# Clamps of four more weight pieces on GpSimd, and the third tile's products of r and k written ahead of the first weight piece

## The chip, the cores and the metric

The program runs on one core of one Trainium2 chip. The metric is the device time of one execution in microseconds (us). The engines are TensorE (PE; PEld is its weight load), VectorE (DVE), ScalarE (ACT), GpSimd (POOL) and SyncE (SP), whose queue issues the DMAs.

## The reference

Three layers follow each other, all in float32, on batch 4 and sequence 768.

```python
# 1: linear attention with a decaying state, per head (8 heads of 48)
for t in range(S):
    cur = einsum('bhd,bhe->bhde', u * k[t], v[t])
    y[t] = einsum('bhd,bhde->bhe', r[t], state + cur)
    state = w * state + einsum('bhd,bhe->bhde', k[t], v[t])
# 2: MLP 384 -> 1024 -> 384 with a 3-tap convolution over time as gate
h = maximum(x @ w_in, 0)
conv_out = sum(conv_w[k] * shifted(h, k) for k in range(3))
x = (h * sigmoid(conv_out)) @ w_out
# 3: layer norm, MLP 384 -> 1536 -> 384, residual
xn = (x - mean) / sqrt(var + 1e-6) * g_ln
out = x + maximum(xn @ w_ch1, 0) @ w_ch2
```

## The kernel before, in words

The 3072 rows are cut into 24 tiles of 128. For a tile, attention scales r and k by tables of powers of w (`rk`), forms scores on TensorE (`dps`), copies them on ScalarE (`aT`) and masks them (on GpSimd for the first six tiles, which are "light"), and multiplies by v into `yps`. For light tiles VectorE also forms `z`, the product of r and k, of which TensorE makes `pa`. A running state (`pst`, `sn`, `sw`, `sbds`) goes from tile to tile, and `kks` are k's scaled rows for it. The output is split into a rounded high part (`xh`, ScalarE) and a remainder (`xl`, VectorE). Three tiles make a block of 384 rows for the first MLP (`moe1_up`, products `psm` and `acc`, eight channel blocks each); `xh` and `xl` need one column of the next tile too, so the first block waits for the fourth tile. The second MLP runs on blocks of 512 rows after that.

All products of the MLPs use three float32r matmuls: high by high, high by low, low by high. The weights must first be split into such halves, piece by piece (22 pieces, a list `wjobs`): a piece `st` of 512 or 768 columns is loaded, ScalarE takes the absolute value of the upper words (`wdec`, in `magnitude`), a **clamp** follows, then VectorE shifts (first step of `decode`), merges twice, ScalarE writes the high part (`wih`, `woh`) and VectorE the low part (`wil`, `wol`). Piece numbers count from 0 in the code: 0 to 2 and 4 to 6 are of `w_in` (512 columns), 3 and 7 to 9 of `w_out` (768), from 10 on those of the second MLP. The clamp's engine is chosen in `ahead` (line 155): VectorE for pieces 0 to 9, GpSimd for the others. `ahead` of the next piece is called when the merges of a piece have been written, so its absolute value and clamp stand early. `wdo` (line 211) writes the next steps of the decoding at a place of the program.

The scheduler may reorder an engine's work, but instructions that go through the `vo`, `ao`, `go`, `pe` and `so` wrappers (class `InOrder`) keep the order in which they are written, on their own engine. The start is written out by hand in `startup` (line 435): `on(n)` writes the next step of tile n. The steps of a light tile end at the `yield` statements of `attn_tile` and `light_tile`: scaling and `z` on VectorE; scores, selects; output products and the copy `xh`; remainder `xl`. So the third `on(0)` writes TensorE's `yps` of the first tile and ScalarE's `xh`, and the first `on(2)` writes `rk` and `z` of the third tile.

Of the kernel before, what the change touches and what calls it, by code (L numbers as in the profile page):

```python
# [50 lines left out]
def body(ctx, tc, r, k, v, w, u, w_in, conv_w, w_out, g_ln, w_ch1, w_ch2, rkT, krv, small, out):  # L51
# [28 lines left out]
    vo = InOrder(nc.vector)  # L80
    ao = InOrder(nc.scalar)
    so = InOrder(nc.sync)
    go = InOrder(nc.gpsimd)
# [35 lines left out]
    def words(st, n):  # L119
        return [st[:, 0:2 * n].rearrange("p (n two) -> p n two", two=2)[:, :, i] for i in range(2)]  # L120

    def magnitude(st, n, engine=go):

        t = ap.tile([128, WN], F32, tag="wd", name="wdec", bufs=2)[:, 0:n]
        ao.activation(out=t, in_=words(st, n)[1].bitcast(F32), func=AF.Abs)
        engine.tensor_scalar(out=t, in0=t, scalar1=W_MIN, scalar2=W_MAX, op0=ALU.max, op1=ALU.min)
        return t

    def decode(st, n, t):

        lo, hi = words(st, n)
        ti = t.bitcast(I32)
        vo.tensor_scalar(out=ti, in0=ti, scalar1=5, scalar2=2, op0=ALU.logical_shift_left,
                         op1=ALU.logical_shift_right)
        yield
        vo.scalar_tensor_tensor(out=ti, in0=lo, scalar=29, in1=ti, op0=ALU.logical_shift_right, op1=ALU.bitwise_or)
        yield
        vo.scalar_tensor_tensor(out=ti, in0=hi, scalar=-(2 ** 30), in1=ti, op0=ALU.bitwise_and, op1=ALU.bitwise_or)
# [3 lines left out]
    def wjob(src, n, hi, lo, scale=None):  # L142

        st, mag = [], []

        def load():
            st.append(io.tile([128, 2 * WN], I32, tag="st" if me >= 4 else "first", name="st", bufs=3 if me >= 4 else 4))
            dst = st[0][:, 0:2 * n]
            if len(src.shape) == 3:
                dst = dst.rearrange("p (a n) -> p a n", a=src.shape[1])  # L150
            so.dma_start(out=dst, in_=src.bitcast(I32))

        def ahead():
            if not mag:
                mag.append(magnitude(st[0], n, vo if me < 10 else go))

        def steps():
            ahead()
            t = mag[0]
            yield from decode(st[0], n, t)  # L160
            if me + 1 < min(len(wjobs), w_loaded[0]):
                wjobs[me + 1][2]()
            if len(src.shape) == 3:
                t = t.rearrange("p (a n) -> p a n", a=src.shape[1])
            kw = {} if scale is None else {"scale": gl[:, scale:scale + 1]}
            ao.activation(out=hi, in_=t, func=AF.Copy, **kw)
            yield
            if scale is None:
                vo.tensor_tensor(out=lo, in0=t, in1=hi.bitcast(F32), op=ALU.subtract)
            else:  # L170
                vo.scalar_tensor_tensor(out=lo, in0=t, scalar=kw["scale"], in1=hi.bitcast(F32),
                                        op0=ALU.mult, op1=ALU.subtract)
        me = len(wjobs)
        wjobs.append((load, steps(), ahead))
        return len(wjobs) - 1

# [28 lines left out]
    def wload(count):  # L205

        while w_loaded[0] < min(count, len(wjobs)):
            wjobs[w_loaded[0]][0]()
            w_loaded[0] += 1

    def wdo(count=1, last=None):

        for _ in range(count):
            while w_done[0] < (len(wjobs) if last is None else last + 1):
                wload(w_done[0] + 3)
                if next(wjobs[w_done[0]][1], "end") != "end":
                    break
                w_done[0] += 1
# [89 lines left out]
    def ordered(n):  # L308
        return (vo, ao, go) if n < EARLY else (nc.vector, nc.scalar, nc.gpsimd)
# [58 lines left out]
    def attn_tile(n):  # L368
        b, i = divmod(n, TPB)
        rk, _, rt, vt, _ = loaded[n]  # L370
        py, py_tag = (ps_c, "acc") if n < EARLY else (ps_a, "pa")

        rT, kT = rk[:, 0], rk[:, 1]
        vo.tensor_tensor(out=rk, in0=rk, in1=trk, op=ALU.mult)
        if n < LIGHT:
            yield from light_tile(n, rk, vt, py, py_tag)
            return
        av = ap.tile([128, H, D], F32, tag="av", name="av", bufs=2)
        v_.tensor_tensor(out=av, in0=kks[:, n % 2, 1, :, 0:D], in1=rt, op=ALU.mult)
        a8 = sp.tile([128, H, 1], F32, tag="a8", name="a8", bufs=2)  # L380
        v_.tensor_reduce(out=a8.rearrange("x (q p) o -> x q (p o)", q=2), in_=av.rearrange("x (p q) d -> x q p d", q=2),
                         axis=AX.X, op=ALU.add)
        aT = ap.tile([128, 2, NP, C], F32, tag="aT", name="aT", bufs=2)
        for h in range(H):
            a_.activation(out=aT[:, h // NP, h % NP, :], in_=ident, func=AF.Copy, scale=a8[:, h, :])
        yield

        dps = dot_products(rT, kT)
        for q in range(2):
            v_.copy_predicated(out=aT[:, q], mask=later.bitcast(I32).unsqueeze(1).to_broadcast([128, NP, C]), data=dps[q])  # L390
        yield

        yps = py.tile([128, KT, C], F32, tag=py_tag, name="yps")
        products(n, yps, rT, vt, aT)
        j = n // TT
        xh, xl = xT[j] if j in xT else new_xT(j)
        sl = slice(1 + (n % TT) * C, 1 + (n % TT) * C + C)
        a_.activation(out=xh[:, :, sl], in_=yps, func=AF.Copy)
        v_.tensor_tensor(out=xl[:, :, sl], in0=yps, in1=xh[:, :, sl].bitcast(F32), op=ALU.subtract)
        load_tile(n + 3)  # L400
        if n + 2 < NT:
            decayed_k(n + 2)
        halos(n, xh, xl)
        finished[0] = n
        yield
# [3 lines left out]
    def state_sum(n):  # L409
        vt = loaded[n][3]  # L410
        if n % TPB != TPB - 1:
            pst = sums[n] = ps_a.tile([128, NP, D], F32, tag="pa", name="pst")
            for h in range(H):
                q0 = 64 * (h % 2)
                pe.matmul(pst[q0:q0 + 64, h // 2, :], lhsT=kks[:, n % 2, 0, h, :], rhs=vt[:, h, 0:D], start=True,
                          stop=True)

    def state_update(n):
        first, last = n % TPB == 0, n % TPB == TPB - 1
        v_, a_, g_ = ordered(n)  # L420
        if not last:
            pst = sums.pop(n)
            sn = ap.tile([PR, NP, D], F32, tag="sn", name="sn")
            if first:
                a_.activation(out=sn, in_=pst[0:PR], func=AF.Copy)
            else:
                v_.tensor_tensor(out=sn, in0=pst[0:PR], in1=state[0], op=ALU.add)
            if n % TPB < TPB - 2:
                state[0] = ap.tile([PR, NP, D], F32, tag="sw", name="sw")
                v_.tensor_tensor(out=state[0], in0=sn, in1=w128.to_broadcast([PR, NP, D]), op=ALU.mult)  # L430
            sb = sbd[(n + 1) % 2]
            a_.activation(out=sb[0:D, :, 0:D], in_=sn[0:D], func=AF.Copy)
            a_.activation(out=sb[64:PR, :, D:2 * D], in_=sn[64:PR], func=AF.Copy)

    def startup():

        tiles = {n: attn_tile(n) for n in range(EARLY + 1)}

        def on(n):
            next(tiles[n], None)  # L440

        decayed = decayed_k
        on(0), decayed(0), on(0)
        on(1), state_sum(0), state_update(0), decayed(1), on(1), state_sum(1)
        wdo(1)
        on(0), on(2), state_update(1), decayed(2)
        wdo(2)
        on(2), state_sum(2), on(0)
        wdo(1)
        on(1), on(3), state_update(2), decayed(3)  # L450
        wdo(2)
        on(3), state_sum(3), on(1)
        wdo(2)
        on(2), state_update(3)
        wdo(3)
        on(2), on(3)
        wdo(1)
        on(3)
        wdo(1)
        on(4), decayed(4)  # L460
        wdo(3)
        return tiles
# [360 lines left out]

    cst = tables()
    feed = attention(startup())
    for _ in conv_weights(cst):
        pass
# [120 lines left out]
```

## Time and profile before

| | |
|---|---|
| time, three runs | 652.41, 653.33 (median), 654.55 us |
| profiled execution | 653.91 us, span 652.2 us |
| mean granted TensorE clock | 0.975 of full |
| busy over the span | PE 627.9, VectorE 421.7, ScalarE 300.8, GpSimd 81.2 us |
| chain that ended last | PE 84%, VectorE 10%, ScalarE 2%, the rest 1% or less each |
| GpSimd clamps | 13, of which 12 have 768 columns; mean 2749 ns |

The table is read with the span in stages: over the whole span TensorE is the fullest engine (96%), but this is a mean over stages. Times in the rows below are microseconds from the start of the span.

### The profile page before, as it was taken

The page shows a single profiled execution, that of the slowest core. Times are in us where ns is not written, and L with a number is a line of the kernel's source. Part 1 is how long each engine was busy: PE and PEld are TensorE (multiplying, and loading weights), DVE is VectorE, ACT ScalarE, POOL GpSimd, SP SyncE. Part 2 cuts the span into 40 slices and gives each one's busy share as a digit, 9 for nine tenths or more (in the row PEclk, how much of TensorE's full clock was granted, in tenths as well). Part 3 has the DMA queues.
Part 4 walks back from the last instruction along what each step waited for, and adds up shares of the span by engine and source line. Part 5 has one row for each costly group of instructions (what it writes and reads, how often), then busy time and mean ns, then how long its engine had stood idle before and what let it go on. Part 6 is the DMA issues. An engine that isn't in the chain of part 4 may idle for free.

```text
span 652.2 us, 11821 instructions
## 1 busy us (share of the span) xinstructions
PE 627.9 (96%) x4803; PEld 572.3 (88%) x4803; DVE 421.7 (65%) x793; ACT 300.8 (46%) x658; POOL 81.2 (12%) x108
## 2 busy tenths in 40 slices
PE   8969879999999999999999999999999999999996
PEld 5768868889999999999999999999999999999995
DVE  6989999999989999968978834314213422422111
ACT  3447677687687877766755511211211211211110
POOL 6312010110020001002115501001000100100000
PEclk8867989999999999999999999999999999999999
DMA  8934644444253524012125103002002001100001
GB/s 231 309 107 156 211 146 125 125 133 159 71 174 118 162 83 137 18 47 88 52 82 171 60 0 98 1 0 98 1 0 83 16 0 50 50 0 19 31 0 54
DMA packets 25296, 56.52 MB, mean 87 GB/s; under 512 B 2961, under 2 KB 15378, under 8 KB 25234
## 3 DMA queue, kind: packets, MB, share of 16 engines
q1 hardware_dynamic: 25234, 55.68, 27.1%
q8 instruction: 40, 0.66, 0.4%
q14 instruction: 22, 0.18, 0.1%
HBM read 46.24 MB, written 9.44 MB: 85 GB/s over the span
## 4 chain that ended last, share of the span: by engine, by line
PE 84%; DVE 10%; ACT 2%; issue 1%; DMA 1%; POOL 1%; SPq 0%; DVEq 0%; ACTq 0%; POOLq 0%
PE acc L77 36%; PE psm L77 36%; PE yps L77 5%; PE dps L77 4%; DVE wdec L77 3%; DVE c L541 2%; PE pst L77 2%; PE pxt L77 1%; DVE rk L77 1%; DMA x1b<-x_dram 1%; DVE c L522 1%; PE pa L77 1%; DVE gl L528 1%; DVE kks L77 0%; POOL tables L762 0%
## 5 line engine op out<-in xcount | busy, mean ns | idle before, releaser
L555 DVE SCALAR_TENSOR_TENSOR rl<-psm,rh 128x512 fp32r<-128x512 f32 x72 | 49.6, 689 | 136.0 <-ACT rh L554 132.5
L554 ACT ACTIVATE rh<-psm 128x512 fp32r<-128x512 f32 x72 | 43.1, 599 | 199.6 <-PE psm L77 199.5
L77 PE MATMUL acc<-c2h,rh 128*128 128x384 f32 x288 | 97.0, 337 | 0.0
L77 PE MATMUL acc<-c2l,rh 128*128 128x384 f32 x288 | 97.0, 337 | 0.0
L77 PE MATMUL acc<-c2h,rl 128*128 128x384 f32 x288 | 96.9, 336 | 0.0
L77 PE MATMUL psm<-xnh,c1h 128*128 128x512 f32 x216 | 86.6, 401 | 0.0
L77 PE MATMUL psm<-xnh,c1l 128*128 128x512 f32 x216 | 84.9, 393 | 0.0
L77 PE MATMUL psm<-xnl,c1h 128*128 128x512 f32 x216 | 84.7, 392 | 0.0
L541 DVE SCALAR_TENSOR_TENSOR c<-h,tables,c 128x384 f32<-128x384 f32 x128 | 78.5, 617 | 8.0 <-ACT c L539 7.5
L77 PE MATMUL psm<-xh,wih 128*128 128x386 f32 x192 | 69.8, 364 | 4.4 <-DVE xl L77 4.4
L77 PE MATMUL acc<-woh,gl 128*128 128x384 f32 x192 | 65.3, 340 | 4.4 <-DVE gl L528 4.4
L77 PE MATMUL acc<-woh,gh 128*128 128x384 f32 x192 | 67.4, 351 | 0.4 <-ACT gh L527 0.4
L77 PE MATMUL psm<-xl,wih 128*128 128x386 f32 x192 | 67.1, 350 | 0.0
L77 PE MATMUL psm<-xh,wil 128*128 128x386 f32 x192 | 66.9, 348 | 0.0
L77 PE MATMUL acc<-wol,gh 128*128 128x384 f32 x192 | 65.3, 340 | 0.0
L77 PEld LDWEIGHTS acc<-c2l,rh 128*128 128x128 f32 x288 | 54.0, 188 | 3.0
L77 PEld LDWEIGHTS acc<-c2h,rh 128*128 128x128 f32 x288 | 54.1, 188 | 2.8
L77 PEld LDWEIGHTS acc<-c2h,rl 128*128 128x128 f32 x288 | 54.0, 188 | 0.0
L77 PEld LDWEIGHTS psm<-xnh,c1l 128*128 128x128 f32 x216 | 40.6, 188 | 9.3
L77 POOL TENSOR_SCALAR wdec<-wdec 128x768 f32<-128x768 f32 (+1 forms) x13 | 35.7, 2749 | 103.4 <-ACT wdec L77 76.3
L77 PEld LDWEIGHTS psm<-xnl,c1h 128*128 128x128 f32 x216 | 40.6, 188 | 6.1
L77 PEld LDWEIGHTS psm<-xnh,c1h 128*128 128x128 f32 x216 | 40.6, 188 | 6.1
(132 smaller groups left out, 1107.9 us busy)
## 6 DMA issues: line engine op xcount, KB each, us to landing
rk<-in_rkT_dram SPq DMA_DIRECT2D x24, 448.0 KB, 4.5
st<-in_moe_w_ch_dram SPq DMA_DIRECT2D x12, 768.0 KB, 4.6
rv<-in_krv_dram SPq DMA_DIRECT2D x18, 448.0 KB, 4.7
kt<-in_krv_dram SPq DMA_DIRECT2D x24, 192.0 KB, 4.5
x_dram<-x SPq DMA_DIRECT2D x24, 192.0 KB, 1.9
x1b<-x_dram SPq DMA_DIRECT2D x24, 192.0 KB, 3.3
out_dram<-x1b SPq DMA_DIRECT2D x24, 192.0 KB, 2.0
st<-in_moe_w_in_dram SPq DMA_DIRECT2D x6, 512.0 KB, 9.4
```

Source lines behind the costliest of these rows:

```text
L77: return lambda *args, **kw: tc.keep_in_program_order(op(*args, **kw))
L522: v_.tensor_tensor(out=st["c"], in0=st["h"][:, 1:T + 1], in1=st["c"], op=ALU.mult)
L528: v_.tensor_tensor(out=st["gl"], in0=st["c"], in1=st["gh"].bitcast(F32), op=ALU.subtract)
L541: v_.scalar_tensor_tensor(out=c, in0=h[:, o:o + T], scalar=cw[:, tap, f:f + 1], in1=c, op0=ALU.mult, op1=ALU.add)
L554: a_.activation(out=gh[:, 0:cols], in_=ps[:, 0:cols], func=AF.Relu)
L555: v_.scalar_tensor_tensor(out=gl_[:, 0:cols], in0=ps[:, 0:cols], scalar=0.0, in1=gh[:, 0:cols].bitcast(F32), op0=ALU.max, op1=ALU.subtract)
```

## The change

The limit in `ahead` goes from 10 to 6, so that the clamps of pieces 6, 7, 8 and 9 are written for GpSimd. In `startup`, `on(0), on(2)` move from behind `wdo(1)`, which writes the first steps of the first piece, to the place in front of it.

```diff
@@ -152,7 +152,7 @@
 
         def ahead():
             if not mag:
-                mag.append(magnitude(st[0], n, vo if me < 10 else go))
+                mag.append(magnitude(st[0], n, vo if me < 6 else go))
 
         def steps():
             ahead()
@@ -442,8 +442,9 @@
         decayed = decayed_k
         on(0), decayed(0), on(0)
         on(1), state_sum(0), state_update(0), decayed(1), on(1), state_sum(1)
+        on(0), on(2)
         wdo(1)
-        on(0), on(2), state_update(1), decayed(2)
+        state_update(1), decayed(2)
         wdo(2)
         on(2), state_sum(2), on(0)
         wdo(1)
```

**ScalarE and VectorE at the first piece.** In the program before, ScalarE's order from the second tile's column `a8` on (`wdec_338` is the first piece's absolute value, `xh_364` the first tile's output copy):

```order
L77 ACTIVATE a8_321<-pa8_315 128x8
L77 ACTIVATE wdec_338<-st_142 128x512
L77 ACTIVATE xh_364<-yps_342 128x3x128
L77 ACTIVATE sbds_93<-sn_370 48x4x48 x2
L77 ACTIVATE wdec_379<-st_150 128x512
L77 ACTIVATE wih_94<-wdec_338 128x512
```

And in the changed one, where `wdec_366` is the first piece and `xh_360` the first tile's copy:

```order
L77 ACTIVATE a8_321<-pa8_315 128x8
L77 ACTIVATE xh_360<-yps_338 128x3x128
L77 ACTIVATE wdec_366<-st_142 128x512
L77 ACTIVATE sbds_93<-sn_370 48x4x48 x2
L77 ACTIVATE wdec_379<-st_150 128x512
L77 ACTIVATE wih_94<-wdec_366 128x512
```

The absolute value and the copy have changed places. VectorE at the same place before (the first row of `wdec_338`, x2, is its clamp and its shift; `rk_137` and `z` are the third tile's):

```order
L77 TENSOR_TENSOR kks_92<-kt_131,tables_84 128x8x48
L77 TENSOR_SCALAR wdec_338<-wdec_338 128x512 x2
L77 TENSOR_TENSOR rk_137<-rk_137,tables_84 112x1024
L77 TENSOR_TENSOR z_368<-rk_137 112x512
L77 TENSOR_TENSOR sn_370<-pst_329,sw_300 112x192
L77 TENSOR_TENSOR sw_372<-sn_370,w128_87 112x192
L77 TENSOR_TENSOR kks_92<-kt_138,tables_84 128x8x48
L77 SCALAR_TENSOR_TENSOR wdec_338<-st_142,wdec_338 128x512 x2
```

and in the changed program:

```order
L77 TENSOR_TENSOR kks_92<-kt_131,tables_84 128x8x48
L77 TENSOR_TENSOR rk_137<-rk_137,tables_84 112x1024
L77 TENSOR_TENSOR z_364<-rk_137 112x512
L77 TENSOR_SCALAR wdec_366<-wdec_366 128x512 x2
L77 TENSOR_TENSOR sn_370<-pst_329,sw_300 112x192
L77 TENSOR_TENSOR sw_372<-sn_370,w128_87 112x192
L77 TENSOR_TENSOR kks_92<-kt_138,tables_84 128x8x48
L77 SCALAR_TENSOR_TENSOR wdec_366<-st_142,wdec_366 128x512 x2
```

The third tile's two products stand ahead of the clamp; the rest keeps its order.

**GpSimd from the fifth tile's selects on** (L336; `wdec` with 24 columns are the convolution weights, `va` a product of the light tiles), the difference:

```order
 L294 MEMSET xl 128x3
-L336 AFFINE_SELECT aT<-aT 128x512 x2
+L336 AFFINE_SELECT aT<-aT 128x512
 L77 TENSOR_SCALAR wdec<-wdec 128x24
+L336 AFFINE_SELECT aT<-aT 128x512
 L340 TENSOR_TENSOR va<-rv,a_675 128x384
+L77 TENSOR_SCALAR wdec<-wdec 128x512
+L77 TENSOR_SCALAR wdec<-wdec 128x768
 L336 AFFINE_SELECT aT<-aT 128x512 x2
 L340 TENSOR_TENSOR va<-rv,a_824 128x384
-L77 TENSOR_SCALAR wdec<-wdec 128x768
+L77 TENSOR_SCALAR wdec<-wdec 128x768 x3
```

Four clamps have come in, two of them ahead of the sixth tile's selects, and the small clamp of the convolution weights has moved between the fifth tile's two selects.

**TensorE at the fifth tile's scores** (`dps_659`), behind the first channel block's products. TensorE's order is the same in both programs up to the end of the first MLP; what differs here is what the first score waits for. Before:

```order
L77 MATMUL psm_630<-xl_365,wih_94 128x386
L77 MATMUL psm_630<-xh_364,wil_95 128x386
L77 MATMUL dps_659<-rk_157 128x128 [waits DMAHW1_49,DVE_49,Activation_49]
L77 MATMUL dps_660<-rk_157 128x128
L77 MATMUL dps_659<-rk_157 128x128
```

and now:

```order
L77 MATMUL psm_630<-xl_361,wih_94 128x386
L77 MATMUL psm_630<-xh_360,wil_95 128x386
L77 MATMUL dps_659<-rk_157 128x128 [waits DMAHW1_49,DVE_49]
L77 MATMUL dps_660<-rk_157 128x128
L77 MATMUL dps_659<-rk_157 128x128
```

It no longer waits for ScalarE. Behind all this the scheduler also gives VectorE another order of its work on the first MLP's first three blocks, with the same instructions.

## Rows read from the trace of the kernel before

**Rows 1.** Busy time by stage: us, then busy time of each engine (instructions), PEclk, DMA share, GB/s.

```profile
50.00:90.00 40.00, 33.60 (x313) 30.70 (x313) 39.51 (x65) 31.14 (x66) 7.04 (x6) 0.93 0.50 157
90.00:123.00 33.00, 31.25 (x395) 27.96 (x395) 31.14 (x56) 23.92 (x64) 0.91 (x3) 0.95 0.48 145
123.00:290.00 167.00, 165.77 (x1801) 154.40 (x1801) 153.82 (x273) 126.77 (x309) 13.69 (x21) 1.00 0.35 109
```

**Rows 2.** The chain that ended last, at two handovers: start, us, what.

```profile
40.11 3.25 PE psm L77 x9
...
89.21 0.45 DVE gl L528
89.70 2.34 PE acc L77 x7
```

**Rows 3.** VectorE's timeline at the first piece: start, us, what [idle before <-releaser].

```profile
12.65 0.55 DVE L77 TENSOR_TENSOR kks<-kt,tables 128x384 f32<-128x384 f32 x1
16.09 0.99 DVE L77 TENSOR_SCALAR wdec<-wdec 128x512 f32<-128x512 f32 x2 [2.89 <-ACT wdec L77]
17.00 1.22 DVE L77 TENSOR_TENSOR rk<-rk,tables 112x1024 f32<-112x1024 f32 x1
...
18.93 0.35 DVE L77 TENSOR_TENSOR sn<-pst,sw 112x192 f32<-112x192 f32 x1
```

**Rows 4.** ScalarE's timeline at the same place.

```profile
15.38 0.68 ACT L77 ACTIVATE wdec<-st 128x512 f32<-128x512 f32 x1
19.65 0.49 ACT L77 ACTIVATE xh<-yps 128x384 fp32r<-128x384 f32 x1 [3.60 <-PE yps L77]
20.04 0.73 ACT L77 ACTIVATE sbds<-sn 48x192 f32<-48x192 f32 x2
```

**Rows 5.** The third tile's `rk`: its issue in SyncE's queue, and landing times of `rk`.

```profile
4.08 0.43 SPq L77 DMA_DIRECT2D rk<-in_rkT_dram  x1
...
DMA to landing us min/median/max: 4.1/9.2/10.5
```

**Rows 6.** VectorE's timeline, two waits between 33 and 49 us.

```profile
35.08 0.56 DVE L77 TENSOR_SCALAR wdec<-wdec 128x768 f32<-128x768 f32 x1 [1.29 <-ACT wdec L77]
...
48.23 0.80 DVE L77 TENSOR_SCALAR wdec<-wdec 128x24 int32<-128x24 int32 x1 [1.48 <-POOL wdec L77]
```

**Rows 7.** TensorE's timeline: scores of the fifth tile, output products of the sixth.

```profile
43.93 2.08 PE L77 MATMUL dps<-rk 48*128 48x128 f32 x16 [0.58 <-ACT h L538]
...
67.51 0.86 PE L77 MATMUL yps<-rk,sbds 112*32 112x128 f32 x24
```

**Rows 8.** GpSimd's timeline from 45 to 90 us.

```profile
46.71 1.23 POOL L336 TENSOR_SCALAR_AFFINE_SELECT aT<-aT 128x512 f32<-128x512 f32 x2 [11.61 <-ACT aT L335]
47.90 0.29 POOL L77 TENSOR_SCALAR wdec<-wdec 128x24 f32<-128x24 f32 x1
...
58.34 2.96 POOL L336 TENSOR_SCALAR_AFFINE_SELECT aT<-aT 128x512 f32<-128x512 f32 x2 [9.35 <-ACT aT L335]
61.27 1.26 POOL L340 TENSOR_TENSOR va<-rv,a 128x384 f32<-128x384 f32 x1
82.48 2.77 POOL L77 TENSOR_SCALAR wdec<-wdec 128x768 f32<-128x768 f32 x1 [19.95 <-ACT wdec L77]
```

**Rows 9.** VectorE's timeline: clamps of pieces 6 to 8.

```profile
52.94 0.42 DVE L77 TENSOR_SCALAR wdec<-wdec 128x512 f32<-128x512 f32 x1
...
61.77 1.18 DVE L77 TENSOR_SCALAR wdec<-wdec 128x768 f32<-128x768 f32 x1
...
68.61 0.55 DVE L77 TENSOR_SCALAR wdec<-wdec 128x768 f32<-128x768 f32 x1
```

**Rows 10.** VectorE's timeline: one product of the gate, alone and beside a GpSimd clamp.

```profile
74.15 0.55 DVE L522 TENSOR_TENSOR c<-h,c 128x384 f32<-128x384 f32 x1
...
82.76 0.96 DVE L522 TENSOR_TENSOR c<-h,c 128x384 f32<-128x384 f32 x1
```

**Rows 11.** Busy time and granted clock behind the wait at 89.70 (columns as in rows 1).

```profile
89.80:93.30 3.50, 3.50 (x12) 3.50 (x13) 3.50 (x7) 2.53 (x7) 0.00 (x0) 0.54 0.86 311
```

## The prediction

> **What bounds the kernel now.** I read the busy time by stage first, then the chain that ended last, then the engines' timelines at the places that the change touches. From 50 to 90 us VectorE is busy 39.51 of 40 us while TensorE has 33.60; from 90 to 123 both are close to full (31.14 and 31.25 of 33); from 123 to 290 TensorE works 165.77 of 167 [rows 1]. So the first 90 us hang on VectorE and the rest on TensorE. The chain says the same: TensorE's first product of the first MLP starts at 40.11 when VectorE's last halo cast is through, and at 89.70 TensorE goes on when VectorE has written `gl`; from there the chain is TensorE's [rows 2]. What VectorE gains or loses before 90 us therefore moves the end by about as much, since little idle time is left behind it to take it up.
>
> **Part one: the third tile's products and the first piece.** VectorE is free at 12.65 + 0.55 = 13.20 and then idles 2.89 us until 16.09, where ScalarE's absolute value of the first piece releases the clamp; clamp and shift take 17.00 - 16.09 = 0.91; the two products of the third tile then fill 17.00 to 18.93 [rows 3]. Written in front, the two (18.93 - 17.00 = 1.93 us) fit into that idle time: their transfer is issued at 4.08 and the median such transfer takes 9.2 us to land, so about 13.3 [rows 5]. That alone would take 1.93 us off VectorE's queue.
>
> But `on(0)`, which is moved with `on(2)`, issues more than VectorE work. It writes the first tile's output products for TensorE and the copy `xh` for ScalarE, and ScalarE's order is kept: `xh` now stands ahead of the absolute value. Now the absolute value runs at 15.38 for 0.68 us; `xh` waits until 19.65 for TensorE, and the next ScalarE instruction starts at 20.04 [rows 4]. TensorE's order there is unchanged, so `xh` stays at 19.65. After the change the absolute value runs from 20.04 to 20.72, clamp and shift from about 20.75 to 21.66, and the state sum `sn` behind them starts at 21.66 in place of 18.93 [rows 3]: **2.73 us later**. The idle time grows to some 5.5 us where it was to be filled. Behind `sn` stand the keys and the decoding on which TensorE's next tiles wait. Bounds: the idle 1.29 us at 35.08 [rows 6] could take up that much (1.4 left), but it ends on ScalarE behind TensorE work that waited for VectorE, so it moves along; I take 2.73.
>
> Two waits near 45 us go. TensorE's scores of the fifth tile now wait 0.58 us for ScalarE's `h` [rows 7]; in the changed order that wait is gone (another PSUM buffer): -0.6. The small clamp of the convolution weights, for which VectorE idles 1.48 us at 48.23 [rows 6], now stands on GpSimd behind both selects, which take 1.23 us together, and starts at 47.90 [rows 8]; in the new order it stands behind the first: half of 1.23, -0.6. If VectorE's own lateness hides them, neither counts; bounds 0 and -1.2. I take both, as both lie on the chain that releases 48.23. After 50 us the change stands at 2.73 - 1.2 = **+1.5**.
>
> **Part two: four clamps.** The four VectorE instructions that go took 0.42, 1.18, 0.55 and once more 0.55 us [rows 9] (the fourth repeats the third and isn't shown). Neighbours overlap by some 0.08 us, so the short three free 0.34 + 0.47 + 0.47. The 1.18 is a 0.55 that ran beside GpSimd's product at 61.27 [rows 8]; that work stays and would stretch whatever stands there, so I count 0.47: together **-1.75**, with -2.4 if the stretch goes too. They lie in the stage in which VectorE is full, so they count in full.
>
> GpSimd takes 2.77 us for such a clamp [rows 8], and about 1.85 for the one of 512 columns (in proportion, an estimate). It has 7.0 us of work between 50 and 90 [rows 1], and each absolute value is written one piece ahead: 2.77 us is well under the 7 to 9 us that lie between a piece's old clamp and the next one's [rows 9], so I cost the wait at nothing; if a shift did come up early, 2 us each at most. The selects of the sixth tile at 58.34 come to stand behind a clamp and may start up to 2.8 us later; with the product behind them they ended at 62.53, and TensorE's output products of that tile start at 67.51 [rows 7, 8], so 5 us cover it.
>
> Beside a GpSimd clamp VectorE loses something. While GpSimd ran the clamp of 82.48, one VectorE product took 0.96 us instead of 0.55 [rows 8, 10], and what followed ran on. That is 0.41 per clamp as an upper bound of the ordinary case and nothing as the lower; I take half, 0.2, as only one instruction of several was hit: **+0.8** for four (0 to 1.6). The Trainium skill (SBUF — State Buffer, section Who interferes with whom) says that VectorE and GpSimd share a port pair as an exclusive lock, held for the whole instruction, and that the second to come fully blocks. The trace does not agree with so long a hold: VectorE worked on inside those 2.77 us. By the page the sum would be some 9 us worse.
>
> **Behind 90 us** VectorE's order is shuffled by the scheduler; TensorE has 33 - 31.25 = 1.75 us of idle time there [rows 1], and the last piece's decoding now comes a little sooner. Between 0 and -1.75 I take a third, **-0.6**.
>
> **Sum:** +1.5 - 1.75 + 0.8 - 0.6 = -0.05, no change. The profiled execution took 653.91 us (span 652.2); the median of the three runs is 653.33, 0.58 below it. I forecast against the median: **653.4**. The likeliest case alone lies between 652.2 and 655.0.
>
> **Rivals.** *Faster by a clock stretch:* from 89.80 to 93.30 TensorE was granted 0.54 of its clock, most of it the 1.2 GHz level [rows 11], right behind its wait for `gl` at 89.70 [rows 2]. At 2.4 GHz the same work needs 3.5 x 0.54 = 1.9 us: 1.6 back. If VectorE reaches `gl` sooner against TensorE's work, the idle time shrinks and the stretch may stay at full speed. With no contention and the stretched 1.18 gone too, -0.05 - 1.6 - 0.8 - 0.65 = -3.1: 650.3. For it: the four clamps stand just ahead of `gl`. Against: VectorE arrives there still late from part one. Chance 0.17.
>
> *Faster as meant:* ScalarE isn't held up by `xh` and part one gains its 1.93: with both waits and the part behind 90 us as in the sum, 653.3 - 1.93 - 1.2 - 1.75 + 0.8 - 0.6 = 648.6. ScalarE's kept order speaks against it; 0.03.
>
> *Slower:* the loss of part one isn't paid back. This decides if GpSimd stretches a VectorE instruction by 0.41 for every clamp (+1.6) and the two waits at 45 us bring nothing because VectorE is the last to arrive there: 2.73 - 1.75 + 1.64 = +2.6, and with nothing regained behind 90 us 655.9. For it: the select and product of GpSimd at 58.34 to 62.5 cost VectorE 0.63 in one instruction, more than a clamp did [rows 8, 9]. Against: VectorE after 90 us has some slack [rows 1]. Chance 0.20.
>
> *Much slower:* VectorE is kept out for whole clamps: 3 x 2.77 + 1.85 = 10.2 in place of 0.8, 663. The instruction that ran through a clamp [rows 10] speaks against it; 0.03. This is the lock of the Trainium skill's page SBUF — State Buffer, section Who interferes with whom; here the trace disagrees.
>
> **How the numbers follow.** A difference under 0.3% (2.0 us) can't be told from no change by a measurement of this kernel. No change 0.57; faster 0.17 + 0.03 = 0.20; slower 0.20 + 0.03 = 0.23. The range takes in most of the first rival and the slower one: 651.0 to 656.3.
>
> **What would show it.** Right: VectorE's idle time ahead of the first clamp is 5 to 6 us and ends on ScalarE's absolute value, which follows `xh`; TensorE's first MLP product starts near 42.8 instead of 40.11; `gl` at 89.70 comes within 1.5 us of its old time; four more GpSimd clamps of 1.9 to 2.8 us and no VectorE wait for them over 0.5 us. Wrong: a first clamp near 16 us (then it is faster); a VectorE that idles for GpSimd between 50 and 90 us; VectorE instructions of 2 us beside a clamp; a granted clock that differs between 90 and 94 us, which alone is worth 1.6 us.

## The result, and the profile after the change

| | before | changed |
|---|---|---|
| median time (7 runs each) | 654.55 us (652.41 to 656.21) | 658.23 us (657.43 to 660.45) |
| ratio, 95% interval | | 1.0066 (1.0049 to 1.0083) |
| profiled execution, span | 653.91 us, 652.2 us | 658.62 us, 656.8 us |
| mean granted TensorE clock | 0.975 | 0.966 |
| busy: PE, VectorE, ScalarE, GpSimd | 627.9, 421.7, 300.8, 81.2 us | 632.9, 423.8, 301.0, 93.1 us |

The change makes the kernel **slower by 0.66%, some 4.3 us**. The forecast was no change (653.4, range 651.0 to 656.3), and the measured time lies above that range. VectorE's busy time rose, although four instructions left it.

ScalarE's timeline of the changed kernel at the first weight piece (start, us, what, idle time before it and its releaser):

```profile
21.14 0.49 ACT L77 ACTIVATE xh<-yps 128x384 fp32r<-128x384 f32 x1 [5.25 <-PE yps L77]
21.65 0.68 ACT L77 ACTIVATE wdec<-st 128x512 f32<-128x512 f32 x1
```

and VectorE's:

```profile
13.35 1.85 DVE L77 TENSOR_TENSOR rk<-rk,tables 112x1024 f32<-112x1024 f32 x1
15.30 0.93 DVE L77 TENSOR_TENSOR z<-rk 112x512 f32<-112x512 f32 x1
22.36 0.89 DVE L77 TENSOR_SCALAR wdec<-wdec 128x512 f32<-128x512 f32 x2 [6.13 <-ACT wdec L77]
23.17 0.35 DVE L77 TENSOR_TENSOR sn<-pst,sw 112x192 f32<-112x192 f32 x1
```

Against [rows 3, 4]: `xh` came at 21.14 and not at 19.65, the absolute value behind it at 21.65 and not at 15.38, and the state sum `sn` at 23.17 in place of 18.93, **4.24 us late**. VectorE's idle time of 2.89 us has grown to 6.13.

TensorE's timeline: the first products of the first MLP, what it waited for up to 90 us, and a product with the sixth `gl`:

```profile
43.48 0.66 PE L77 MATMUL psm<-xh,wih 128*128 128x386 f32 x1 [5.27 <-DVE xl L77]
...
46.64 2.08 PE L77 MATMUL dps<-rk 48*128 48x128 f32 x16
...
62.52 1.82 PE L77 MATMUL pa<-ub,z 112*128 112x2 f32 x8 [1.95 <-DVE z L77]
...
86.61 2.08 PE L77 MATMUL dps<-rk 48*128 48x128 f32 x16 [2.71 <-issue]
...
95.14 0.34 PE L77 MATMUL acc<-woh,gl 128*128 128x384 f32 x1
```

The first MLP starts 3.37 us late (43.48 against 40.11 [rows 2]), so 0.87 of the 4.24 us had been made up ahead of it: VectorE's idle time of 1.29 us at 35.08 [rows 6] has shrunk to 0.56. The two waits that I expected to go did go: the scores at 46.64 have no idle time ahead of them (0.58 in [rows 7]), and VectorE waits 0.18 us for the small clamp (1.48 in [rows 6]). VectorE's timeline there, with the copy of the convolution weights to `tables` that ends this stage:

```profile
50.74 0.59 DVE L77 TENSOR_SCALAR wdec<-wdec 128x24 int32<-128x24 int32 x1 [0.18 <-POOL wdec L77]
...
52.39 0.18 DVE L789 COPY tables<-wdec 128x24 f32<-128x24 f32 x1
```

and the copy in the kernel before:

```profile
49.50 0.18 DVE L788 COPY tables<-wdec 128x24 f32<-128x24 f32 x1
```

It is **2.89 us late**. TensorE then waits twice more. The scores at 86.61 follow VectorE's `rk` of the seventh tile, which ends at 86.51. They came 6.47 us later than in the kernel before. VectorE's timeline ahead of them, and the sixth `gl`:

```profile
81.93 0.54 DVE L379 TENSOR_TENSOR av<-kks,rv 128x384 f32<-128x384 f32 x1
82.40 0.94 DVE L77 TENSOR_TENSOR wol<-wdec,woh 128x768 fp32r<-128x768 f32 x1
83.26 0.55 DVE L77 TENSOR_SCALAR wdec<-wdec 128x768 int32<-128x768 int32 x1
83.73 0.54 DVE L381 TENSOR_REDUCE a<-av 128x8 f32<-128x384 f32 x1
...
85.30 1.21 DVE L77 TENSOR_TENSOR rk<-rk,tables 112x1024 f32<-112x1024 f32 x1
...
92.91 0.55 DVE L529 TENSOR_TENSOR gl<-c,gh 128x384 fp32r<-128x384 f32 x1
```

In the kernel before, the first four of these stand behind that `rk`, and its scores follow it in the same way (`rk` ends at 80.03; ScalarE's `c`, which the view names, ended at 79.65):

```profile
78.82 1.21 DVE L77 TENSOR_TENSOR rk<-rk,tables 112x1024 f32<-112x1024 f32 x1
```

```profile
80.14 1.16 PE L77 MATMUL dps<-rk 48*128 48x128 f32 x16 [1.93 <-ACT c L539]
```

Busy time and granted clock of the changed kernel behind these two waits (columns as in [rows 1]):

```profile
59.20:62.50 3.30, 1.38 (x19) 1.07 (x18) 3.30 (x7) 1.87 (x4) 2.04 (x1) 1.00 0.46 187
62.56:69.38 6.82, 6.82 (x24) 6.82 (x25) 6.82 (x11) 4.72 (x11) 3.89 (x5) 0.50 0.34 106
86.45:93.28 6.83, 6.67 (x31) 6.48 (x32) 6.83 (x13) 5.50 (x16) 0.07 (x2) 0.50 0.18 37
```

and of the kernel before at the same places:

```profile
59.35:62.76 3.41, 3.41 (x12) 3.41 (x12) 3.41 (x4) 1.94 (x5) 3.18 (x3) 0.50 0.02 5
90.07:93.48 3.41, 3.41 (x13) 3.41 (x12) 3.41 (x7) 2.26 (x7) 0.00 (x0) 0.50 0.90 329
```

Each stretch at 0.50 (the 1.2 GHz level) is twice as long: 6.8 against 3.4 us. From 97 to 300 us TensorE is 3.3 to 4.1 us behind. By the end it is 4.6 behind; no run was made for what comes behind 300 us.

GpSimd's timeline from 53 to 78 us, and with it the VectorE instructions that ran beside its clamps:

```profile
53.93 1.91 POOL L77 TENSOR_SCALAR wdec<-wdec 128x512 f32<-128x512 f32 x1 [1.84 <-DVE c L542]
60.46 2.85 POOL L77 TENSOR_SCALAR wdec<-wdec 128x768 f32<-128x768 f32 x1 [4.61 <-ACT wdec L77]
63.27 2.10 POOL L336 TENSOR_SCALAR_AFFINE_SELECT aT<-aT 128x512 f32<-128x512 f32 x2
...
69.32 3.21 POOL L77 TENSOR_SCALAR wdec<-wdec 128x768 f32<-128x768 f32 x1 [2.72 <-ACT wdec L77]
74.86 3.21 POOL L77 TENSOR_SCALAR wdec<-wdec 128x768 f32<-128x768 f32 x1 [2.32 <-ACT wdec L77]
```

```profile
60.59 1.18 DVE L542 SCALAR_TENSOR_TENSOR c<-h,tables,c 128x384 f32<-128x384 f32 x1
61.70 0.68 DVE L77 TENSOR_TENSOR z<-rk 112x512 f32<-112x512 f32 x1
62.30 0.60 DVE L542 SCALAR_TENSOR_TENSOR c<-h,tables,c 128x384 f32<-128x384 f32 x1
...
69.82 1.18 DVE L542 SCALAR_TENSOR_TENSOR c<-h,tables,c 128x384 f32<-128x384 f32 x1
...
75.35 1.58 DVE L77 SCALAR_TENSOR_TENSOR wdec<-st,wdec 128x768 int32<-128x768 int32 x1
```

Beside each clamp one VectorE instruction is long, and those behind it are not: the filter tap `c` takes 1.18 beside the clamp of 60.46, and 0.60 two instructions on. The excess over the usual time of the same form is 0.57, 0.57 and 0.63 here, and 0.39 beside the clamp of 53.93: **2.2 us for the four**. The sixth tile's selects start at 63.27, when the clamp ahead of them ends, and its output products come only at 73.21, so that cover held.

To see what adds up, I counted VectorE's records from the start to the sixth `gl` of the first MLP (at 89.11 in the kernel before; it releases TensorE at 89.70 [rows 2]), and split the difference to the kernel before into three: **idle** time, the **set** of instructions that stand ahead of it (more or fewer, each at the mean time of its kind in the kernel before), and **stretch** (the same instructions, but longer).

| kernel | sixth gl, us | idle | set | stretch |
|---|---|---|---|---|
| changed | +3.80 | +2.01 | -2.01 | +3.81 |
| e1 clamps alone | +2.55 | -0.22 | +0.25 | +2.53 |
| e2 move alone | +7.31 | +2.25 | +3.66 | +1.41 |
| e3 third tile's products alone | +0.47 | -1.31 | 0.00 | +1.78 |
| e4 clamps left out | -0.86 | -1.75 | +0.25 | +0.64 |
| e5 as e1, order held | +0.05 | -1.24 | -1.47 | +2.77 |
| e6 as e4, order held | -0.51 | +0.18 | -1.47 | +0.80 |
| e8 changed, on(0) put back, order held | -1.69 | -4.19 | -1.47 | +3.98 |

The stretch of the changed kernel is more than the four clamps: the two moved products take 1.85 and 0.93 at 13.35 and 15.30, where GpSimd's `va` of the first tile and the selects of the second run beside them, and 1.22 and 0.69 before. One profile each, and the first 30 us depend on where the half-clock stretches fall in that execution, so single entries are good to about 1 us.

In the changed kernel this `gl` is not what TensorE waits for: it is written by 93.46, and its product runs at 95.14. TensorE has waited 2.71 us for the seventh tile's `rk` instead. Counted in the same way up to that `rk` (85.30 against 78.82), the 6.5 us are +2.0 idle, -0.2 set and +4.7 stretch. The four clamps are gone from ahead of it, but the scheduler has put the four instructions shown above in their place. So at the place where TensorE waited, nothing of the saving was left.

### The profile page after: what moved, and what is told of

Same layout as the page of the kernel before. It is cut to its first block, busy times and chain, and to the rows that moved or that the text cites. A ratio compares the mean times of both kernels' runs of the same rounds, so it can differ in the third digit from the quotient of the medians.

```text
span 656.8 us, 11828 instructions
## 1 busy us (share of the span) xinstructions
PE 632.9 (96%) x4803; PEld 576.4 (88%) x4803; DVE 423.8 (65%) x789; ACT 301.0 (46%) x658; POOL 93.1 (14%) x112
## 4 chain that ended last, share of the span: by engine, by line
PE 80%; DVE 12%; issue 3%; DMA 2%; ACT 1%; POOL 1%; SPq 0%; POOLq 0%; ACTq 0%; DVEq 0%
PE acc L77 35%; PE psm L77 34%; PE yps L77 5%; PE dps L77 3%; DVE wdec L77 3%; DVE c L542 2%; PE pst L77 2%; DMA x1b<-x_dram 2%; DVE rk L77 1%; PE pxt L77 1%; PE pa L77 1%; DVE c L523 1%; DVE gl L529 1%; DVE bs L576 1%; DVE aT L390 0%
## 5 line engine op out<-in xcount | busy, mean ns | idle before, releaser
L542 DVE SCALAR_TENSOR_TENSOR c<-h,tables,c 128x384 f32<-128x384 f32 x128 | 80.2, 631 | 7.3 <-ACT c L540 6.8
L77 POOL TENSOR_SCALAR wdec<-wdec 128x768 f32<-128x768 f32 (+2 forms) x17 | 47.6, 2800 | 98.8 <-ACT wdec L77 64.6
```

The source lines that it names most:

```text
L77: return lambda *args, **kw: tc.keep_in_program_order(op(*args, **kw))
L542: v_.scalar_tensor_tensor(out=c, in0=h[:, o:o + T], scalar=cw[:, tap, f:f + 1], in1=c, op0=ALU.mult, op1=ALU.add)
```

## The experiments

The theories on record: A, the loss is the late first piece, because ScalarE's kept order puts `xh` ahead of the absolute value. B, it is the clamps on GpSimd (stretched VectorE instructions, late selects). C, neither alone, but half-clock stretches that only both together bring on. The first results added D: the scheduler's order of VectorE. All times are against runs of the kernel before on the same chip.

### Each part alone

e1: the clamps go, the start is written as before.

```diff
-                mag.append(magnitude(st[0], n, vo if me < 10 else go))
+                mag.append(magnitude(st[0], n, vo if me < 6 else go))
```

> The four clamps go to GpSimd, the start is written as before. Theory A (the start carries the loss: ScalarE takes the first tile's output copy ahead of the first piece's absolute value, and everything behind comes some 3 us later): without the move this kernel is 0 to 1.5 us faster than before, because VectorE is rid of 1.75 us of clamps and pays back part of it beside GpSimd. Theory B (the clamps carry it: each GpSimd clamp stretches a VectorE instruction by about 0.6 us, and the sixth tile's selects stand behind a clamp): 2 to 4 us slower than before. Theory C (the two parts are worth little alone; together they lengthen half-clock stretches of TensorE): within 1 us of before, and so is the move alone.

Measured: 657.20 against 654.17, ratio 1.0048 (1.0032 to 1.0064): some 3.1 us slower.

e2: only the move.

```diff
+        on(0), on(2)
         wdo(1)
-        on(0), on(2), state_update(1), decayed(2)
+        state_update(1), decayed(2)
```

> The clamps stay on VectorE, on(0) and on(2) stand in front of the first piece. Theory A: 3 to 5 us slower than before, the whole loss; the first weight clamp on VectorE comes near 22.4 us as in the changed kernel, TensorE's first MLP product near 43.5 us. Theory B: within 1 us of before. Theory C: within 1 us of before, with the half-clock stretch behind 62 us of 3.4 us, not of 6.8 us.

Measured: 661.80, ratio 1.0101 (1.0068 to 1.0134), 657.18 to 665.41: some 6.6 us slower, more than the whole change. C is out, for either part loses by itself, and the parts do not add. From about 55 us on e2 also has another VectorE order than the kernel before (set +3.66 in the table), so this run can't tell the late first piece from the order.

e3: only the third tile's products in front.

```diff
+        on(2)
         wdo(1)
-        on(0), on(2), state_update(1), decayed(2)
+        on(0), state_update(1), decayed(2)
```

> Only on(2), the third tile's products, stands in front of the first piece; on(0), with the output copy, stays behind it; clamps stay on VectorE. Theory A: ScalarE's absolute value stays near 15.4 us, the two products fill VectorE's idle time, the first clamp comes near 16.2 us; 0 to 2 us faster than before. Theory B says nothing of this one beyond 'not slower'. If moving the products alone loses as much as the move of both, ScalarE's order is not the cause.

Measured: 654.87, ratio 1.0009 (0.9995 to 1.0023): no change that can be told. In the start the engines' orders of e2 and e3 differ only in ScalarE's pair. ScalarE's timeline of e3:

```profile
14.54 0.70 ACT L77 ACTIVATE wdec<-st 128x512 f32<-128x512 f32 x1 [0.43 <-DMA st<-in_moe_w_in_dram]
16.82 0.49 ACT L77 ACTIVATE xh<-yps 128x384 fp32r<-128x384 f32 x1 [1.59 <-PE yps L77]
```

and VectorE's:

```profile
15.32 0.93 DVE L77 TENSOR_TENSOR z<-rk 112x512 f32<-112x512 f32 x1
16.18 1.19 DVE L77 TENSOR_SCALAR wdec<-wdec 128x512 f32<-128x512 f32 x2
17.29 0.34 DVE L77 TENSOR_TENSOR sn<-pst,sw 112x192 f32<-112x192 f32 x1
```

Here the products do fill the idle time and `sn` comes 1.64 us early (17.29 against 18.93 [rows 3]). The gain is not seen at the end, although VectorE's order is that of the kernel before but for the two products. Theory A expected a gain of 0 to 2 us.

e9: only `on(0)` in front.

```diff
+        on(0)
         wdo(1)
-        on(0), on(2), state_update(1), decayed(2)
+        on(2), state_update(1), decayed(2)
```

> Only on(0), with the first tile's output copy on ScalarE, stands in front of the first piece; the third tile's products stay behind it and the clamps on VectorE. Theory A (ScalarE's order is the loss of the move): slower than before by 5 to 9 us, as much as the move of both (6.6) or up to 2 us more, since the products now wait behind the late piece too. If it is within 2 us of before, the two have to be moved together for the loss, and theory A is incomplete.

Measured: 663.30 against 654.86, ratio 1.0157 (1.0115 to 1.0200), 660.44 to 668.63: `on(0)` alone carries the loss of the move, and theory A holds for it. How large the loss gets is not fixed at the start: `sn` was only 1.87 late in this profile (20.80). TensorE then waited 2.52 us for a `gl` at 64.78 and 4.55 for the sixth at 94.79, with 10.2 us at half clock around the second.

### The clamps left out, and VectorE's order

e4: the start of before, no clamps on pieces 6 to 9.

```diff
-        engine.tensor_scalar(out=t, in0=t, scalar1=W_MIN, scalar2=W_MAX, op0=ALU.max, op1=ALU.min)
+        if engine is not None:
+            engine.tensor_scalar(out=t, in0=t, scalar1=W_MIN, scalar2=W_MAX, op0=ALU.max, op1=ALU.min)
...
-                mag.append(magnitude(st[0], n, vo if me < 10 else go))
+                mag.append(magnitude(st[0], n, None if 6 <= me < 10 else vo if me < 6 else go))
```

> Start as before; the clamps of the seventh to tenth piece are left out altogether (that part of the computation is missing). It shows what VectorE's 1.75 us are worth if nothing runs on GpSimd in their place. Theory A: 1 to 2 us faster than before, and at most 1 us faster than the kernel with the clamps on GpSimd. Theory B: 1 to 2 us faster than before and 3 to 5 us faster than the kernel with the clamps on GpSimd. Theory C: 0 to 1 us faster.

Measured: 654.95 against 654.17, ratio 1.0014 (1.0000 to 1.0028). Taking 1.75 us off VectorE and putting nothing in its place gains nothing. VectorE's timeline of e1 (e4 has the same order) suggests why:

```profile
89.79 0.54 DVE L522 TENSOR_TENSOR c<-h,c 128x384 f32<-128x384 f32 x1
90.25 0.34 DVE L430 TENSOR_TENSOR sw<-sn,w 112x192 f32<-112x192 f32 x1
90.52 1.21 DVE L77 TENSOR_TENSOR rk<-rk,tables 112x1024 f32<-112x1024 f32 x1
91.66 0.54 DVE L528 TENSOR_TENSOR gl<-c,gh 128x384 fp32r<-128x384 f32 x1
```

In the kernel before `gl` stands at 89.11 and a gate product, `sw` and `rk` of the eighth tile behind it. With four instructions fewer the scheduler, which may move `gl`, puts these three ahead of it. So the freed time goes to a tile that nobody waits for yet, and the set ahead of the gl is +0.25 us in place of about -2 (table). That is theory D; e5 to e7 test it.

e5: e1, with `sw` and `rk` held behind the sixth `gl`.

```diff
+        with tc.issue_after(gls[5].ins) if n == 7 else nullcontext():
             vo.tensor_tensor(out=rk, in0=rk, in1=trk, op=ALU.mult)
...
+                with tc.issue_after(gls[5].ins) if n == 6 else nullcontext():
                     v_.tensor_tensor(out=state[0], in0=sn, in1=w128.to_broadcast([PR, NP, D]), op=ALU.mult)
```

> The clamps alone on GpSimd, and the state product sw and the product rk of the eighth tile held behind the sixth gl on VectorE, as they stand in the kernel before. Theory D (the scheduler's order: with four instructions less the scheduler puts these two, 1.5 us, and a gate product ahead of the gl for which TensorE waits): about 2 us faster than the clamps alone, within 1.5 us of before. Theory B (only the stretch beside GpSimd counts): no faster than the clamps alone, 2 to 4 us over before.

Measured: 655.49 against 653.89, ratio 1.0017 (1.0002 to 1.0032). VectorE's timeline shows `gl` ahead of both, and TensorE goes on at 89.76 where in e1 it was 92.25:

```profile
89.16 0.54 DVE L530 TENSOR_TENSOR gl<-c,gh 128x384 fp32r<-128x384 f32 x1
89.63 0.34 DVE L432 TENSOR_TENSOR sw<-sn,w 112x192 f32<-112x192 f32 x1
89.90 1.21 DVE L77 TENSOR_TENSOR rk<-rk,tables 112x1024 f32<-112x1024 f32 x1
```

The order was worth 0.31% (1.0048 to 1.0017), 2.0 us, as D expected; the two intervals just touch.

e6: e4, held in the same way.

> The four clamps left out altogether (that part of the computation is missing), with the same order of VectorE as the run beside it. The difference to that run is what the GpSimd clamps cost by being run at all: by the stretch read from the traces (some 0.5 us for each of four) 2 us. Theory D: 1 to 2.5 us faster than before, since the freed 1.75 us now reach the gl. If it is not faster than before, VectorE's time ahead of the sixth gl is not what sets the end.

Measured: 653.82 against 653.89, ratio 0.9989 (0.9973 to 1.0006). The two kernels' VectorE orders are the same, so 1.0017 - 0.9989 = 0.28%, **1.8 us, is what four clamps cost by running on GpSimd** (e1 against e4: 0.34%, 2.2 us). The ratios' intervals overlap slightly, but the twelve times of each run, from the same chip, have means 1.85 us apart, with a 95% interval of about 1.0 either way. Against the kernel before, e6 gains only 0.11%, 0.7 us, which cannot be told from nothing. D expected 1 to 2.5 us here, so holding the two instructions did not bring VectorE's freed 1.75 us to the end. What the clamps cost on GpSimd is therefore at least as much as the kernel gains by being rid of them on VectorE.

e7: e2, held in the same way, with the next two gate products behind the `gl` as well.

```diff
+        with tc.issue_after(gls[5].ins) if len(gls) in (6, 7) else nullcontext():
             v_.tensor_tensor(out=st["c"], in0=st["h"][:, 1:T + 1], in1=st["c"], op=ALU.mult)
```

> The move alone, with sw, rk and the two next gate products held behind the sixth gl. Theory D: the move alone lost 3.7 us of its 7 to the order of VectorE ahead of that gl; pinned it should lose 3 to 4.5 us against before, what the late first piece costs by itself. If it loses 6 or more, the order was not the cause.

Measured: 661.80 against 653.89, ratio 1.0110 (1.0089 to 1.0131): no gain, D fails here. TensorE's wait stands elsewhere:

```profile
95.21 0.69 PE L77 MATMUL acc<-woh,gh 128*128 128x384 f32 x1 [5.89 <-ACT gh L531]
```

ScalarE's timeline:

```profile
93.91 0.84 ACT L77 ACTIVATE woh<-wdec 128x768 fp32r<-128x768 f32 x1
94.65 0.51 ACT L531 ACTIVATE gh<-c 128x384 fp32r<-128x384 f32 x1
```

The gate product behind which `gh` comes was done only at 93.76, which is most of the wait, and `gh` then still stands behind the tenth piece's `woh` (0.84 us) on ScalarE. The order that helped e5 did not help here.

### The change, undone in one place

e8: the change with `on(0)` put back, order held as in e5. The edit is shown against the kernel before. (In the change itself `sw` and `rk` stand behind that `gl` anyway, and holding them there alters no row of its VectorE order.)

```diff
+        on(2)
         wdo(1)
-        on(0), on(2), state_update(1), decayed(2)
+        on(0), state_update(1), decayed(2)
...
-                mag.append(magnitude(st[0], n, vo if me < 10 else go))
+                mag.append(magnitude(st[0], n, vo if me < 6 else go))
```

> As the change but with on(0) left behind the first piece, and with sw and rk held behind the sixth gl. Theories A and D together: neither the late first piece nor the order is left, only the stretch beside GpSimd against the 1.75 us of the clamps; within 1.5 us of before and 3 us or more faster than the change.

Measured: 654.56 against 653.89, ratio 1.0014 (0.9998 to 1.0029). Against the change's 1.0066 that is 0.52%, **3.4 us for `on(0)` ahead of the first piece**, with what the scheduler makes of it behind 50 us, where VectorE's order differs too. The 0.9 us that are left can't be told from no change. Its sixth `gl` came 1.69 us early, and from 90 us on TensorE was 1.4 to 2.1 us ahead of the kernel before, up to 143 us, but none of that reached the end: at 141.66 it waited 1.38 us, and 3.4 us at half clock followed. (The kernel before waits 1.23 us at 143.53, with no such stretch.) Against e5, whose VectorE order is the same but for the two products, e8 is not faster either (1.0014 and 1.0017).

e10: the change with the four clamps left out. It has the holds of e5 too; VectorE's order is row for row that of the change.

```diff
-                mag.append(magnitude(st[0], n, vo if me < 6 else go))
+                mag.append(magnitude(st[0], n, None if 6 <= me < 10 else vo if me < 6 else go))
```

> The change with the four GpSimd clamps left out (that part of the computation is missing); VectorE's order is that of the change, word for word. Theory B: each clamp costs VectorE some 0.5 us, 2.0 us for the four; this kernel should be 1.5 to 3 us faster than the change, 1 to 3 us slower than before. If it is as slow as the change, the clamps cost nothing where they run and the whole loss is the late first piece.

Measured: 657.48 against 654.86, ratio 1.0051 (1.0031 to 1.0071). That is 1.0 us below the change, but the intervals overlap, so the share of the clamps inside the change is not shown by this run. Most of the loss remains without them. In its profile TensorE waits 2.85 us for the scores of the same tile at 83.65, as in the change.

### Two tries for a faster kernel

e11 is e8, and e12 the kernel before, each with `rk` of tiles 9 and 10 free for the scheduler. Tiles count from 0 here. The scores that wait near 121 us are tile 10's, but those near 142 us are tile 12's, so the edit does not touch that wait, and the expectation for it goes untested.

```diff
-            vo.tensor_tensor(out=rk, in0=rk, in1=trk, op=ALU.mult)
+            (nc.vector if n in (9, 10) else vo).tensor_tensor(out=rk, in0=rk, in1=trk, op=ALU.mult)
```

> As the run with the products in front, the clamps on GpSimd and the pinned gl, and the products rk of tiles 9 and 10 free for the scheduler, which puts them some 20 us ahead of the scores that wait for them (1.1 and 1.4 us of TensorE's idle time at 121 and 142 us). If those waits bring on the half-clock stretch behind 143 us, it goes with them: 1.5 to 4 us faster than that run, and faster than before. If VectorE's earlier work only makes other gl late, no change or slower.

Measured: 655.80 against 654.86, ratio 1.0019 (1.0000 to 1.0039). The wait at 121 us is gone, and TensorE waits 1.00 us at 107.15 instead. Tile 12's scores still wait, behind an `rk` that ends at 145.56, and longer than in e8 (1.38):

```profile
145.66 1.16 PE L77 MATMUL dps<-rk 48*128 48x128 f32 x16 [2.10 <-issue]
```

> The kernel before with the products rk of tiles 9 and 10 free for the scheduler, nothing else. If the waits at 122.8 and 143.5 us (0.97 and 1.23 us) cost what they last, 1 to 2 us faster than before; if they are made up behind 145 us or other gl come late, within 1 us of it.

Measured: 656.48, ratio 1.0029 (1.0012 to 1.0045), slower. TensorE now waits 1.55 us at 104.09 and 2.31 at 142.87 (tile 12 again), with 6.8 us at half clock behind. No version of this study beats the kernel before.

## Why the prediction was wrong

**What bounds the kernel** was right for lateness: up to 90 us VectorE's lateness is TensorE's, and it moves the end. For a gain it isn't shown: e6 and e8 had the sixth `gl` 0.51 and 1.69 us early, and neither was faster than the kernel before.

**Part one, the mechanism** was right and shown (e3 against e2, e9, e8 against the change): ScalarE takes `xh` first, and the first piece waits for TensorE. **Its size was the first step that failed:** I put the lateness behind 50 us at +1.5, and VectorE's `tables` copy came 2.89 us late. "TensorE's order there is unchanged, so `xh` stays at 19.65" took the time of one execution for that of the program. The order was unchanged, but from 16 to 20 us TensorE was granted 0.50 of its clock in the changed profile and 0.70 before, and `xh` came at 21.14. In e10, which starts as the change does, the clock was 0.82 there and `xh` came at 18.28, `sn` at 20.30. So a part of the 4.24 us belongs to that one execution. What holds over the profiles is the `tables` copy: it starts between 48.48 and 49.94 in the six programs with the start of before, and between 51.43 and 53.00 in the five with `on(0)` in front. The two waits paid back 0.5 (3.37 us late ahead of them, 2.89 behind) and not 1.2; the idle time at 35.08, which I let move along, took up 0.9.

**Part two, the saving** was there at the sixth `gl` (set -2.01, I had -1.75). **That it counts in full was the second step that failed:** in the changed kernel TensorE waits for `rk`, ahead of which the set is as large as before (-0.2), and with the clamps left out and the order held (e6) the kernel is faster by 0.7 us, which is not clear of noise. **The price beside GpSimd was the third:** I took 0.2 for each clamp and 0.41 as the upper end, from one row [rows 8, 10], and the traces show 0.39, 0.57, 0.57 and 0.63. With the measured terms the sum at the sixth `gl` is +2.9 - 2.0 + 2.2 = +3.1, and 0.61 us of a new wait of VectorE at 73.01 for ScalarE's `woh`, which I had not foreseen, makes it +3.7; measured is +3.80. That this is close to the 4.3 us at the end is luck, since TensorE does not wait there. The part behind 90 us (-0.6) did not come.

**What I left out** is the order: that fewer VectorE instructions make the scheduler put others ahead of the one that TensorE waits for. In the change they stand ahead of `rk`, in e1 ahead of the `gl`, where they cost 2.0 us. I had put the shuffling behind 90 us and read it as harmless; it begins near 55 us. Likewise lateness was carried to the end with a surcharge (twice 3.4 us more at half clock), while the lead of e8 was not.

**The rivals.** "Slower, part one not repaid" was the case that came, at 0.20; its price of 655.9 was too small, since it took over 2.73 and 0.41. Of its two conditions the stretch held (and more); the other held in part, for both waits went but paid back 0.5. The clock rival named the right place with the wrong sign: the stretch there got longer, not shorter. "Faster as meant" assumed that ScalarE isn't held up; e3, where it isn't, shows no gain either.

**The stated signs:** VectorE's idle time ahead of the first clamp 6.13 (said 5 to 6, "ends on ScalarE's absolute value": yes); first MLP product at 43.48 (said 42.8); `gl` within 1.5 us of its old time: no, 3.80, and TensorE's wait had moved to `rk`; four clamps of 1.91 to 3.21 us (said 1.9 to 2.8); no wait of VectorE for them over 0.5 us: right, the longest is 0.2.

**Open:** how much of the 3.4 us of `on(0)` is the late first piece and how much the other VectorE order that comes with it, since no run has the one without the other. Also why the move alone is 2 to 3 us slower than the move with the clamps. The set in the table (two more gate products, a `wol` and `rk` ahead of the gl, and the clamps) points to the order, but holding the gl in e7 didn't bring it back, and no run set ScalarE's `gh` ahead of `woh`.

## What to carry to other kernels

Moving a step means moving what it writes on every engine: where an engine's order is kept, a copy that waits for TensorE holds back all that is written behind it. Here that cost 3.4 us, together with the order that the scheduler then chose. An instruction moved to GpSimd beside a full VectorE still costs VectorE time: here 1.8 us for four, where leaving them out altogether gained 0.7 us, not clear of noise. Leaving the instruction out, in the same order, measures that price. With a scheduler, look first whether the freed time goes to the instruction that is waited for: compare the orders ahead of it, not only the sums.

## What the runs showed of the hardware

Beside a full VectorE a GpSimd clamp can take far longer than VectorE loses by it. GpSimd's timeline of e5:

```profile
56.74 5.15 POOL L77 TENSOR_SCALAR wdec<-wdec 128x768 f32<-128x768 f32 x1 [4.48 <-ACT wdec L77]
...
72.21 8.08 POOL L77 TENSOR_SCALAR wdec<-wdec 128x768 f32<-128x768 f32 x1 [4.16 <-ACT wdec L77]
82.12 2.77 POOL L77 TENSOR_SCALAR wdec<-wdec 128x768 f32<-128x768 f32 x1 [1.83 <-ACT wdec L77]
```

VectorE's timeline inside the one of 8.08 us:

```profile
74.71 1.21 DVE L77 TENSOR_TENSOR rk<-rk,tables 112x1024 f32<-112x1024 f32 x1
75.84 0.95 DVE L77 SCALAR_TENSOR_TENSOR wdec<-st,wdec 128x768 int32<-128x768 int32 x1
76.72 0.94 DVE L77 TENSOR_TENSOR kks<-kt,tables 128x768 f32<-128x768 f32 x1
77.58 1.17 DVE L543 SCALAR_TENSOR_TENSOR c<-h,tables,c 128x384 f32<-128x384 f32 x1
```

Clamps of one form take 2.77, 5.15 and 8.08 us here, and they come again at the same pieces in e1 and e8 (2.77, 5.13 and 8.07 in both). In the long ones VectorE runs at its usual pace until one `c` takes 1.17 in place of 0.60, and the clamp ends 2.7 us after the start of that `c` (77.58 to 80.29; in the other 59.19 to 61.89). So it looks as if GpSimd got in only there, and from then on both ran; that is argued from the times, and why it would be at that instruction no run shows. The Trainium skill (SBUF — State Buffer, section Who interferes with whom) says that the second of the two to come fully blocks until the first is done. The traces go with that for GpSimd, whose clamp took up to 5.3 us longer than the shortest (8.08 against 2.77), and not for VectorE, which lost at most 0.63 per clamp and worked on inside it. That loss is steady: in e1, e5 and e8 the clamp of 512 columns stretches one VectorE instruction by 0.45 or 0.46 us, and each of the three with 768 columns that moved stretches one by 0.57.
